# A gated linear recurrence with a convolution-gated output: deeper ring of decays, one gate tile less in flight, gated inputs on GpSimd, other written-out orders

## The chip, the cores and the metric

The kernel runs on one core of a Trainium2 chip. A core has five engines that work at the same time, each through its own queue in order: TensorE (PE, matrix products and transposes), VectorE (DVE), ScalarE (ACT), GpSimd (POOL) and SyncE (SP), which here only issues data transfers (DMAs). They work on a memory of 128 partitions (SBUF); matrix products land in eight banks of a second memory (PSUM). The metric is the device time of one execution in microseconds, as the median of several runs.

## The reference, cut to what matters

```python
# first part: x, r_gate, i_gate are (4, 6336, 256), a_param is (256,)
a_base = sigmoid(a_param)
a_t    = exp(8.0 * sigmoid(r_gate) * log(clip(a_base, 1e-6, 1 - 1e-6)))
norm   = sqrt(maximum(1.0 - a_t * a_t, 1e-6))
xg     = norm * sigmoid(i_gate) * x
h = 0
for t in range(S):                 # for each of the 4 sequences, each of 256 channels
    h = a_t[:, t] * h + xg[:, t]
    y[:, t] = h
# second part, on y
gate_pre[t] = sum(conv_w[k] * y[t - 4 + k] for k in range(5))   # zero before a sequence starts
out = (sigmoid(gate_pre) * (y @ w_val)) @ w_out                 # both weights are 256 x 256
```

## The kernel before, in words

The 4 x 6336 = 25344 tokens are one long row. It is cut into 51 tiles of 512 tokens (three of 256: the first and the last two) and into 28 chunks, nearly all of two tiles, so 1024 tokens; chunk c holds tiles 2c - 2 and 2c - 1. Every sigmoid is written as a tanh: sigmoid(z) = (1 + tanh(z/2)) / 2, so tanh and exp share one activation table, and only the square root needs another. Chunks are therefore taken in pairs (UNITS): one table load, one root for the pair, one table load back.

A tile goes through these steps; the name is the one in the planner, the letter the one in the written-out orders:

- `load` (l, SP, line 264): two DMAs of 512 KB, r_gate and i_gate, into a tile `ri` of a pool with NIN buffers. `loadx` (x, line 271): one DMA of x into `xt`, NX buffers. Both are issued on SP, as the stores are.
- `tanh` (t, ACT, line 348): both gates at once, into `tring`, which has NTR = 3 slots for r and NTI = 5 for i.
- `srT` (r, PE, line 373), per chunk and half of the channels: transposes of tanh(r) into a PSUM bank, so that channels lie on partitions. `exp` (e, ACT, line 382): the decay a_t, into `aring`, a ring of NS windows of 512 tokens.
- `e` (e, POOL, line 390): a_t squared, into `ering`. `sq` (q, ACT, line 394): the root, for a whole unit.
- `u2` (u, line 359 on DVE or lines 363 and 364 on POOL): the gated input (1 + tanh(i/2)) * x, into `uring`. On DVE it is two instructions of 128x512 that each read `tring` and `xt`; on POOL it is an add into `t1` and a product. The string U2 says which engine does which tile.
- `nT` (n, PE, line 404): transposes of the root back to tokens on partitions; `xg` (x, DVE, line 411): root times gated input; `xT` (x, PE, line 420): transposes to channels on partitions.
- `scan` (s, DVE, line 438), per chunk and half: the recurrence, reading `aring` and the bank, into `yring`.
- `conv` (c, PE, line 464): the convolution as products with diagonal matrices; `tg` (g, ACT, line 472): tanh of it; `val` (v, PE, line 480): y @ w_val; `gv` (v, DVE, line 490): their product; `out` (o, PE, line 502), two pieces per tile; `osb` (o, line 513 on DVE or 515 on ACT, by the string OSB): eviction of a piece; `store` (s, SP, line 520).

What each step waits for is written in `make_jobs` (lines 132 to 180), with a cost for each step. The lines on which ring depths act:

```python
        job("load", "DMA", f, [("tanh", g - NIN)])
        job("loadx", "DMA", f, [("u2", g - NX)])
        job("tanh", "ACT", f, [("load", g), ("u2", g - NTI)]
            + ([("srT", 2 * sh.chunk_of[g - NTR] + 1)] if g >= NTR else []))
...
            aold = ("scan", 2 * sh.aold[c] + h if sh.aold[c] >= 0 else -1)
            job("exp", "ACT", f, [("srT", k), aold])
            job("e", "POOL", f, [("exp", k), ("sq", eu), ("nT", sh.chunks[ed][3] - 1 if ed >= 0 else -1)])
```

`sh.aold[c]` is the last earlier chunk whose place in `aring` chunk c takes; with NS = 10 that is five chunks of 1024 back. The order of the work on each engine is not found while the kernel is built: it is written out as one string of letters per engine (ORDER), and BANK_ORDER gives the PSUM bank (one of four) of each srT, nT, xT and out in turn. `make_plan` walks the strings with the costs only to merge the five queues into one program order; on the chip each engine follows its own string, and waits for the others by semaphores.

Of the kernel before, what the change touches and what calls it, by code (L numbers as in the profile page):

```python
# [15 lines left out]

CHUNKS = [[256], [512]] + [[512, 512]] * 23 + [[512], [256], [256]]

UNITS = [2, 2, 2, 2, 2, 2, 2, 2, 2, 2, 2, 2, 2, 2]
NS = 10  # L20
NE = 10
NU = 10
NY = 6
NIN = 4
NX = 4
NTR = 3
NTI = 5
# [2 lines left out]
BANKS = 4  # L30
PB = dict(srT=2, nT=2, xT=2, ops=2)

OSB = "DDDDDDDDDDDDDDDDDDDDDDDDDDDDDDDDDDDDDDDDDDDDDDDDDDDDDADDDDDDDDDDDDDDDDDDDDAAAAADDDDDAAAAAAAAAAADADA"

U2 = "DDDDPDPDDPPPPPPPPPPPDPPPPPPPPPPPPPPPPPPPPPPPPPPPPPP"

COST = dict(load=(0.05, 2.72), loadx=(0.02, 1.37), tanh=(0.11, 1.7), u2P=(0.2, 3.25), u2D=(0.2, 1.7), srT=(0.05,
            0.47), exp=(0.26, 0.86), e=(0.06, 1.83), sq=(0.2, 1.71), nT=(0.05, 0.53), xg=(0.02,
            0.58), xT=(0.04, 0.46), scan=(0.13, 2.14), conv=(0.15, 1.08), tg=(0.1, 0.83), val=(0.02,
            0.88), gv=(0.07, 1.07), out=(0.02, 0.43), osbD=(0.6, 0), osbA=(0.5, 0), store=(0.03,  # L40
# [3 lines left out]
LETTERS = dict(  # L44
    DMA=dict(l="load", x="loadx", s="store"), ACT=dict(t="tanh", e="exp", q="sq", g="tg", o="osb"),
    PE=dict(r="srT", n="nT", x="xT", c="conv", v="val", o="out"), POOL=dict(e="e", u="u2"),
    DVE=dict(u="u2", x="xg", s="scan", v="gv", o="osb"))
ORDER = dict(
    DMA=("lllxlllxlxlxxlxlxxlllxxlxlxsxxlsxlxllssxxlslxsxsllxxlsxssllslsxxxlsllssxslxlslsxxsllxslxslsxxsxslllx"
         "slxsxssllxlxxsxsslslxllsxsxsxllsxslxssxsxxsssssssssss"),  # L50
    ACT=("teeteetqtteteetetgqteegtteettgqgetegetetgqgteegttgetegtgeqgteetgetgqgetettgeegtgqeegttgtegetgtegqegt"
         "tgeetgtegqegttegetgoetgqegttegetgqgetegtgetgetgqeogetgootgoeoteegeqgeogeoqogogoogogooooggoo"),
    PE=("rrrrrrnxnrxrcxvxrcvrnnxnrxrnoocxxvcornrnvnocorxronvcxvooxcxronnvrocnovxncrvxroocxrocvooxvocrononcxrn"
        "voroxconvxocvornonnrcvonxrxvorcoxocovroxvxcrvnooncooxvrocxrvocnnoorcoovxcoorvnxvonocrxvrocoxvnrocono"
        "vxoxcrvonnocxrrxvoocnnrxcovroxovconvonnxrxcrnovcxroocvoxooovcrnnonxocxrvcrvoncovoxocovronxvrnncxnovo"
        "cxroovxrrcorovxoocovnonrcxrovonxcxnnvxocovocxxovcoxovooxcovcovoo"),
    POOL="eeeeeeeeueueeeuuueeeeuuuueeeueuuueeeeuueeeeuuueeuueeuueueueeueueueueeuueueeuuueeueeuuueueeeeuueeeuu",
    DVE=("uxsuxsussuvxuxusxsvxooussovxxvxoosxovsvoosoxxsovoxvxssoovsoovosovooxxusxvoosoxvsooxoxvxvxossovoosoov"
         "svsxooxvoosvosoxovoxoovsoovxsoxvosvoosovxoxovossxxovossoxxvsovosovxooxvxssxovsoovoosoovxxoxsovsvxoov"
         "oosovxsxxvsxvsvsoovoosoxxvsvxsxxvssvssvsvsovvo"))  # L60
BANK_ORDER = ("2123321110130102331302130221230122302301230123012121132131023123012102312123210310103201301301320131"
              "2023103130123102130231201213202310203123132010303132031321023031231202302001302313021231120312310321"
              "20131232130321320112030212312010312032010301231210212310312231")

WEIGHTS_AFTER = ("e", 1)
TABLE, SEM, DMA_LAT = 1.3, 0.15, 2.2
# [2 lines left out]
BF16 = mybir.dt.bfloat16  # L69
ACT = mybir.ActivationFunctionType  # L70
ALU = mybir.AluOpType


class Shape:
# [3 lines left out]
    def __init__(self, total, seq):  # L78
# [9 lines left out]
        assert t == total  # L88
        self.apos, self.aold = self.place(NS * WIN)
        self.epos, _ = self.place(NE * WIN)  # L90
# [3 lines left out]
        self.runs, self.npos, batch_of = [], [], []  # L94
        for u, n in enumerate(UNITS):
            runs = []
# [35 lines left out]
def make_jobs(sh):  # L132
# [4 lines left out]
    jobs = {op: [] for ops in LETTERS.values() for op in ops.values()}  # L137
    unit_of = [u for u, n in enumerate(UNITS) for _ in range(n)]
    ends = [sum(UNITS[:u + 1]) for u in range(len(UNITS))]
    qlast = [max(q for q, (w, _) in enumerate(sh.pieces) if w == g) for g in range(len(sh.tiles))]  # L140

    def job(op, eng, f, deps, cost=None, bank=0):
        fix, per = COST[cost or op]
        jobs[op].append((eng, fix + per * f, [d for d in deps if d[1] >= 0], bank))

    for g, (_, n) in enumerate(sh.tiles):
        f = n / WIN
        c = sh.chunk_of[g]
# [4 lines that stand above are left out]
        job("u2", "DVE" if U2[g] == "D" else "POOL", f, [("tanh", g), ("loadx", g)] + ([("xT", 2 * sh.chunk_of[g - NU] + 1)] if g >= NU else []), "u2" + U2[g])  # L153
        job("nT", "PE", f, [("sq", unit_of[c]), ("xg", g - PB["nT"])], None, 1)
        job("xg", "DVE", f, [("nT", g), ("u2", g)])
        job("conv", "PE", f, [("scan", 2 * c + 1), ("tg", g - 1)])
        job("tg", "ACT", f, [("conv", g), ("gv", g - 2)])
        job("val", "PE", f, [("scan", 2 * c + 1), ("gv", g - 1), ("conv", g)])
        job("gv", "DVE", f, [("tg", g), ("val", g)] + ([("out", qlast[g - 2])] if g >= 2 else []))
        job("store", "DMA", f, [("osb", q) for q, (w, _) in enumerate(sh.pieces) if w == g])  # L160
    for c, (_, n, g0, g1) in enumerate(sh.chunks):
# [3 lines left out]
        for h in range(2):  # L165
            k = 2 * c + h
            job("srT", "PE", f, [("tanh", g1 - 1), ("exp", k - PB["srT"])], None, 1)
# [3 lines that stand above are left out]
            job("xT", "PE", f, [("xg", g1 - 1), ("scan", k - PB["xT"])], None, 1)  # L171
            job("scan", "DVE", f, [("xT", k), ("val", ylast - 1), ("conv", ylast)])
    for q, (g, i) in enumerate(sh.pieces):
        job("out", "PE", 1, [("gv", g), ("osb", q - PB["ops"])], None, 1)
        job("osb", "DVE" if OSB[q] == "D" else "ACT", 1, [("out", q), ("store", g - NOSB)], "osb" + OSB[q])
    for u, n in enumerate(UNITS):
        size = sum(sh.chunks[c][1] for c in range(ends[u] - n, ends[u])) / CHUNK
        fix, per = COST["sq"]
        jobs["sq"].append(("ACT", fix * len(sh.runs[u]) + per * size, [("e", 2 * ends[u] - 1)], 0))
# [3 lines left out]
def make_plan(sh):  # L183
# [5 lines left out]
    for eng, letters in ORDER.items():  # L189
        todo = {op: [i for i, job in enumerate(jobs[op]) if job[0] == eng] for op in LETTERS[eng].values()}  # L190
        seq[eng] = [(op, todo[op].pop(0)) for op in (LETTERS[eng][x] for x in letters)]
        assert not any(todo.values())
    free_bank = iter(BANK_ORDER)
    for op, i in seq["PE"]:
# [5 lines left out]
    done, order, mode = {}, [], "E"  # L200
    free = dict(dict.fromkeys(seq, 0.0), DMA=START, ACT=ACT_START)
    at, left = dict.fromkeys(seq, 0), sum(len(ops) for ops in seq.values())
    while left:
        was = left
        for eng, ops in seq.items():
            while at[eng] < len(ops):
# [9 lines left out]
                free[eng] = t + dur  # L216
                done[op, i] = t + dur + (DMA_LAT if eng == "DMA" else 0.0)
                order.append((t, op, i, eng, dur))
# [8 lines left out]
def kernel(  # L227
# [31 lines left out]
    def load(g):  # L259
        t0, nt = tiles[g]  # L260
        nj = nt // P
        ri = inp.tile([P, 2, SUB, D], FP32, name="ri", tag="ri", bufs=NIN)
        for k, src in enumerate((rf, if_)):
# [10 lines left out]
    with tc.manual_schedule():  # L274
# [51 lines left out]

        aring = rings.tile([P, H, NS * WIN], FP32, name="aring")

# [241 lines left out]
```

## Time and profile before

| what | value |
|---|---|
| time, median of 5 runs | 311.66 us (310.82 to 314.27) |
| the profiled execution | 313.02 us, of it span from first to last instruction 311.2 us |
| ACT busy | 289.1 us |
| DVE busy | 271.6 us |
| PE busy | 249.7 us |
| POOL busy | 243.8 us |
| moved by DMA | 104.51 MB, 336 GB/s over the span |
| granted TensorE clock, mean | 0.962 |

The profile is of one execution. Its page gives the busy time of each engine, then groups of instructions by line, engine and tile with the idle time before them, and what ended that idle time. In a row such as `out<-in 128x1024 f32` the tiles written and read stand ahead of their shape. Rows of the timeline give start, duration, engine and line; two neighbouring instructions of one kind are merged (x2). Consecutive ACT rows overlap by about 0.1 us[...]. "issue" as a releaser means that the profile shows nothing that the engine waited for. Idle time of an engine costs nothing by itself; it counts where another engine, or the end, waits for it.

### The profile page before, as it was taken

How to read it: one execution, taken by the hardware profiler on the slowest of the kernel's cores; microseconds unless marked ns; L12 is line 12 of the kernel's file. 1: busy time of each engine (PE TensorE's matmuls, PEld its weight loads, DVE VectorE, ACT ScalarE, POOL GpSimd, SP SyncE). 2: the span in 40 equal slices, each digit the busy share in tenths (PEclk: the TensorE clock that was granted, in tenths of full speed). 3: DMA queues.
4: the chain of work that ended last, by engine and by line, in shares of the span. 5: the costliest groups of instructions: out<-in, count | busy, mean ns of one | idle time of the engine just before them, and what ended most of it. 6: DMA issues, size and time to landing. Idle time of an engine off the chain costs nothing.

```text
span 311.2 us, 6605 instructions
## 1 busy us (share of the span) xinstructions
PE 249.7 (80%) x2591; PEld 162.5 (52%) x2591; DVE 271.6 (87%) x279; ACT 289.1 (93%) x225; POOL 243.8 (78%) x154
## 2 busy tenths in 40 slices
PE   1126564799799868989799899888897999999994
PEld 1115243465566445655566466555564766656563
DVE  3008957989999998999999999999999999999973
ACT  6799699999999995999999999999999999999762
POOL 1907719999998998548999999999999989987300
PEclk9999796979899995999999999999999999999999
DMA  7999989999898999599999999997989999673145
GB/s 200 385 372 389 400 311 413 395 349 414 293 358 319 379 347 409 197 353 420 384 331 358 359 419 417 414 417 275 393 316 336 368 418 412 238 263 136 70 181 227
DMA packets 30797, 104.51 MB, mean 336 GB/s; under 512 B 4391, under 2 KB 4654, under 8 KB 30766
## 3 DMA queue, kind: packets, MB, share of 16 engines
q1 hardware_dynamic: 29376, 103.82, 88.1%
q0 software_dynamic: 1376, 0.26, 1.0%
q8 instruction: 20, 0.33, 0.4%
q14 instruction: 11, 0.09, 0.1%
q10 hardware_dynamic: 14, 0.01, 0.0%
HBM read 78.39 MB, written 25.95 MB: 335 GB/s over the span
## 4 chain that ended last, share of the span: by engine, by line
ACT 30%; POOL 15%; issue 14%; DVE 14%; PE 14%; DMA 11%; SPq 1%; ACTq 0%; DVEq 0%; POOLq 0%
ACT tring L348 8%; POOL uring L364 8%; ACT ering L394 6%; ACT aring L382 5%; ACT tg L472 5%; DMA ri<-in_i_gate_dram 5%; DMA xt<-in_x_dram 5%; DVE yring L438 5%; PE gp L464 4%; POOL ering L390 4%; POOL t L363 4%; PE bank L502 3%; DVE gv L490 3%; ACT L394 2%; DVE uring L359 2%
## 5 line engine op out<-in xcount | busy, mean ns | idle before, releaser
L390 POOL TENSOR_TENSOR ering<-aring 128x1024 f32<-128x1024 f32 (+2 forms) x56 | 95.5, 1719 | 41.0 <-ACT aring L382 39.2
L438 DVE TENSOR_TENSOR_SCAN yring<-aring,yring,bank 128x1024 bf16<-128x1024 f32 (+5 forms) x54 | 109.9, 2048 | 3.4 <-PE bank L420 3.4
L364 POOL TENSOR_TENSOR uring<-t,xt 128x1024 bf16<-128x1024 f32 (+1 forms) x43 | 100.0, 2327 | 3.6
L348 ACT ACTIVATE tring<-ri 128x2048 bf16<-128x2048 f32 (+1 forms) x51 | 94.2, 1867 | 4.2 <-issue 2.6
L464 PE MATMUL gp<-yring,diag 64*64 64x512 bf16 (+15 forms) x1196 | 67.6, 354 | 1.3 <-ACT tg L472 0.7
L382 ACT ACTIVATE aring<-bank,khf 128x1024 f32<-128x1024 bf16 (+2 forms) x56 | 61.0, 1109 | 4.1 <-PE bank L373 3.4
L502 PE MATMUL bank<-wo,gv 128*128 128x256 bf16 x396 | 58.7, 276 | 6.5 <-DVE osb L513 2.1
L490 DVE SCALAR_TENSOR_TENSOR gv<-tg,val 128x1024 bf16<-128x1024 bf16 (+1 forms) x54 | 60.3, 1120 | 3.2 <-PE val L480 2.5
L373 PE MATMUL bank<-ident_b,tring 128*128 128x128 bf16 x396 | 36.4, 240 | 27.0 <-ACT tring L348 19.1
L472 ACT ACTIVATE tg<-gp 128x1024 bf16<-128x1024 f32 (+1 forms) x51 | 51.3, 1006 | 5.1 <-PE gp L464 4.3
L480 PE MATMUL val<-yring,wv 128*128 128x512 bf16 (+1 forms) x204 | 52.4, 380 | 3.1 <-DVE gv L490 3.0
L513 DVE TENSOR_SCALAR osb<-bank 128x512 f32<-128x512 f32 x80 | 52.4, 676 | 2.3 <-PE bank L502 2.1
L502 PEld LDWEIGHTS <-gv 128*128 128x128 bf16 x396 | 36.8, 99 | 24.1 <-issue 10.1
L373 PEld LDWEIGHTS <-tring 128*128 128x128 bf16 x396 | 29.5, 108 | 35.2 <-ACT tring L348 20.7
L411 DVE TENSOR_TENSOR uring<-bank,uring 128x1024 bf16<-128x1024 bf16 (+1 forms) x51 | 33.4, 664 | 16.2 <-PE bank L404 15.8
L394 ACT ACTIVATE ering<-ering,b 128x4096 bf16<-128x4096 f32 (+4 forms) x16 | 46.8, 2934 | 0.2
L363 POOL TENSOR_SCALAR t<-tring 128x1024 f32<-128x1024 bf16 (+1 forms) x43 | 45.0, 1047 | 1.7
L404 PE MATMUL bank<-ident_f,ering 128*128 128x128 f32 x198 | 36.1, 311 | 11.4 <-ACT ering L394 3.7
L464 PEld LDWEIGHTS <-diag 64*64 64x64 bf16 x1196 | 30.0, 109 | 27.4 <-issue 12.5
L404 PEld LDWEIGHTS bank<-ident_f,ering 128*128 128x128 f32 x198 | 28.5, 208 | 19.1 <-ACT ering L394 8.0
L420 PE MATMUL bank<-ident_f,uring 128*128 128x128 f32 x198 | 33.6, 289 | 5.1 <-DVE uring L411 2.4
L420 PEld LDWEIGHTS bank<-ident_f,uring 128*128 128x128 f32 x198 | 22.8, 145 | 16.0 <-DVE uring L411 4.4
(32 smaller groups left out, 105.8 us busy)
## 6 DMA issues: line engine op xcount, KB each, us to landing
ri<-in_r_gate_dram SPq DMA_DIRECT2D x48, 512.0 KB, 7.8
ri<-in_i_gate_dram SPq DMA_DIRECT2D x48, 512.0 KB, 8.5
xt<-in_x_dram SPq DMA_DIRECT2D x48, 512.0 KB, 8.6
out_dram<-osb SPq DMA_DIRECT2D x48, 512.0 KB, 6.3
ri<-in_r_gate_dram SPq DMA_DIRECT2D x3, 256.0 KB, 6.1
ri<-in_i_gate_dram SPq DMA_DIRECT2D x3, 256.0 KB, 7.6
xt<-in_x_dram SPq DMA_DIRECT2D x3, 256.0 KB, 5.2
out_dram<-osb SPq DMA_DIRECT2D x3, 256.0 KB, 2.1
```

The costliest lines, as they stand in the source:

```text
L348: nc.scalar.activation(out=tring[:, r:i + 1:i - r, 0:nj, :], in_=ri[:, :, 0:nj, :], func=ACT.Tanh, scale=0.5)
L364: nc.gpsimd.tensor_tensor(out=u.rearrange("p w d e -> p w e d"), in0=t1.rearrange("p (w e) d -> p w e d", e=2), in1=xt.rearrange("p (w e) ...
L373: nc.tensor.transpose(out=srT[:, col:col + P], in_=tring[:, g % NTR, j, h * P:(h + 1) * P], identity=ident_b[:])
L382: nc.scalar.activation(out=aring[:, h, a0:a0 + nt].rearrange("c (w p j) -> c w p j", p=P, j=nj), in_=live.pop(("srT", k))[:, 0:nt].rearran ...
L390: nc.gpsimd.tensor_tensor(out=ering[:, H * e0 + h * nt:H * e0 + (h + 1) * nt], in0=a, in1=a, op=ALU.mult)
L394: nc.scalar.activation(out=nring[:, 2 * H * e0:2 * H * e0 + H * m], in_=ering[:, H * e0:H * (e0 + m)], func=ACT.Sqrt, scale=-0.25, bias=b0 ...
L404: nc.tensor.transpose(out=nT[:, w * D + h * P:w * D + (h + 1) * P], in_=ering[:, n0 + w:n0 + nw * P:nw], identity=ident_f[:])
L438: nc.vector.tensor_tensor_scan(out=yring[:, h, y0 + c0:y0 + c1], data0=aring[:, h, a0 + c0:a0 + c1], data1=xT[:, c0:c1], initial=0.0 if fr ...
L464: nc.tensor.matmul(out=gp[64 * h:64 * h + 64, m, c0:c1], lhsT=diag[rows, h, kk, rows], rhs=yring[rows, h, src:src + c1 - c0], start=(sh == 0),
L472: nc.scalar.activation(out=tg[:, :, 0:nt], in_=live.pop(("gp", g))[:, :, 0:nt], func=ACT.Tanh, scale=0.5)
L490: nc.vector.scalar_tensor_tensor(out=gv[:, 0:nj, hs, :].rearrange("c j h p -> c j (h p)"), in0=tg[:, hs, 0:nt].rearrange("c h (p j) -> c j ...
L502: nc.tensor.matmul(out=ops[:, e * D:(e + 1) * D], lhsT=gv[:, 2 * i + e, hk, :], rhs=wo[:, hk, :], start=(hk == 0), stop=(hk == H - 1))
```

## The change

Six constants and the order strings are replaced. No instruction's form changes.

- NS from 10 to 12: `aring` holds 1024 tokens more. NIN from 4 to 3: one tile of gates less.
- U2: on DVE were tiles 0, 1, 2, 3, 5, 7, 8 and 20 (D); now tiles 0, 1, 2, 4 and 8.
- UNITS: the last two roots cover 1 and 3 chunks instead of 2 and 2; the last root thus covers 512 + 256 + 256 tokens instead of 256 + 256.
- OSB: 18 evictions on ACT instead of 19, at other pieces.
- The planner's cost of a gated input on DVE, and the strings of all five queues and of the banks.

```diff
@@ -16,12 +16,12 @@
 
 CHUNKS = [[256], [512]] + [[512, 512]] * 23 + [[512], [256], [256]]
 
-UNITS = [2, 2, 2, 2, 2, 2, 2, 2, 2, 2, 2, 2, 2, 2]
-NS = 10
+UNITS = [2, 2, 2, 2, 2, 2, 2, 2, 2, 2, 2, 2, 1, 3]
+NS = 12
 NE = 10
 NU = 10
 NY = 6
-NIN = 4
+NIN = 3
 NX = 4
 NTR = 3
 NTI = 5
@@ -30,11 +30,11 @@
 BANKS = 4
 PB = dict(srT=2, nT=2, xT=2, ops=2)
 
-OSB = "DDDDDDDDDDDDDDDDDDDDDDDDDDDDDDDDDDDDDDDDDDDDDDDDDDDDDADDDDDDDDDDDDDDDDDDDDAAAAADDDDDAAAAAAAAAAADADA"
-
-U2 = "DDDDPDPDDPPPPPPPPPPPDPPPPPPPPPPPPPPPPPPPPPPPPPPPPPP"
-
-COST = dict(load=(0.05, 2.72), loadx=(0.02, 1.37), tanh=(0.11, 1.7), u2P=(0.2, 3.25), u2D=(0.2, 1.7), srT=(0.05,
+OSB = "DDDDDDDDDDDDDDDDDDDDDDDDDDDDDDDDDDDDDDDDDDDDDDDDDDDDDDDDDDDDDDDDDDDDDDDAADADADDDDADDAAAAAAADAAAAADA"
+
+U2 = "DDDPDPPPDPPPPPPPPPPPPPPPPPPPPPPPPPPPPPPPPPPPPPPPPPP"
+
+COST = dict(load=(0.05, 2.72), loadx=(0.02, 1.37), tanh=(0.11, 1.7), u2P=(0.2, 3.25), u2D=(0.3, 3.3), srT=(0.05,
             0.47), exp=(0.26, 0.86), e=(0.06, 1.83), sq=(0.2, 1.71), nT=(0.05, 0.53), xg=(0.02,
             0.58), xT=(0.04, 0.46), scan=(0.13, 2.14), conv=(0.15, 1.08), tg=(0.1, 0.83), val=(0.02,
             0.88), gv=(0.07, 1.07), out=(0.02, 0.43), osbD=(0.6, 0), osbA=(0.5, 0), store=(0.03,
@@ -46,21 +46,22 @@
     PE=dict(r="srT", n="nT", x="xT", c="conv", v="val", o="out"), POOL=dict(e="e", u="u2"),
     DVE=dict(u="u2", x="xg", s="scan", v="gv", o="osb"))
 ORDER = dict(
-    DMA=("lllxlllxlxlxxlxlxxlllxxlxlxsxxlsxlxllssxxlslxsxsllxxlsxssllslsxxxlsllssxslxlslsxxsllxslxslsxxsxslllx"
-         "slxsxssllxlxxsxsslslxllsxsxsxllsxslxssxsxxsssssssssss"),
-    ACT=("teeteetqtteteetetgqteegtteettgqgetegetetgqgteegttgetegtgeqgteetgetgqgetettgeegtgqeegttgtegetgtegqegt"
-         "tgeetgtegqegttegetgoetgqegttegetgqgetegtgetgetgqeogetgootgoeoteegeqgeogeoqogogoogogooooggoo"),
-    PE=("rrrrrrnxnrxrcxvxrcvrnnxnrxrnoocxxvcornrnvnocorxronvcxvooxcxronnvrocnovxncrvxroocxrocvooxvocrononcxrn"
-        "voroxconvxocvornonnrcvonxrxvorcoxocovroxvxcrvnooncooxvrocxrvocnnoorcoovxcoorvnxvonocrxvrocoxvnrocono"
-        "vxoxcrvonnocxrrxvoocnnrxcovroxovconvonnxrxcrnovcxroocvoxooovcrnnonxocxrvcrvoncovoxocovronxvrnncxnovo"
-        "cxroovxrrcorovxoocovnonrcxrovonxcxnnvxocovocxxovcoxovooxcovcovoo"),
-    POOL="eeeeeeeeueueeeuuueeeeuuuueeeueuuueeeeuueeeeuuueeuueeuueueueeueueueueeuueueeuuueeueeuuueueeeeuueeeuu",
-    DVE=("uxsuxsussuvxuxusxsvxooussovxxvxoosxovsvoosoxxsovoxvxssoovsoovosovooxxusxvoosoxvsooxoxvxvxossovoosoov"
-         "svsxooxvoosvosoxovoxoovsoovxsoxvosvoosovxoxovossxxovossoxxvsovosovxooxvxssxovsoovoosoovxxoxsovsvxoov"
-         "oosovxsxxvsxvsvsoovoosoxxvsvxsxxvssvssvsvsovvo"))
-BANK_ORDER = ("2123321110130102331302130221230122302301230123012121132131023123012102312123210310103201301301320131"
-              "2023103130123102130231201213202310203123132010303132031321023031231202302001302313021231120312310321"
-              "20131232130321320112030212312010312032010301231210212310312231")
+    DMA=("lllxxlllxllxxlxxlxlxlxsllxlxsxlxlslxslxxsllsslxxlslxsxlsxxsllsxlxssllxslxlsxlsxxslxssllsxxxslslslxls"
+         "xxsslxllxsxlsxslslxslssxsxlxxslxlslxsxsssxssssxssssss"),
+    ACT=("teteeetqttgeteetegtqetteeetgtgqteetgtegtetgeegqtgtetegetqgetgteegtgqgtgeteetgtegeetgqtgteegtgqegttge"
+         "etgetgqgteegttgeetgeqgetgtgtegetgqetgtegeetgoqogotgetgoeteegeteegqeogqogoogoogogogooogogoo"),
+    PE=("rrrrnnxxcrvrxxrcrrovnnxrxornrcovncxrxorvnncxnvnrocxrvoocroovxrcvxoocnnoovnxrrncoxrvoxooxcvnnrocoxvno"
+        "rrcnoxcovxorvconnoxcovroxvrncnrxocvroorocvooxcxovonnvxrxrconocnovxorcvroxvonconvorocoxvrnxcoovncooxv"
+        "rxoocrnnvoxocrrvconnxrovrooxcovnnxcovnxcoxrcvnrocoovooxvrxcnvonroocorxvrcooxnoovncxxovnnocnroxcvornx"
+        "rcrxvrrocrovoroxvcovnnocooxvxnoocxovoncovxcoxvncxooxvoxocovcovoo"),
+    POOL=("eeeeeeeeuueueeeuuueueueeeueuueeuuueeeeuuuueeueeuueeueeuuueueeeuuueeueeuueueueeuueueeeuuuueueeeeueeeu"
+          "uu"),
+    DVE=("uuxxssssvuuoxxvsosxuvxososvxxsxxovsovooovssovoxooxxsxvosovoossxxvoosxvoxosovsovoxxosovosxvxsoovoovoo"
+         "sovosxxvssooxxovosvosovxoxoovosxvsxoovoososvxxoovosvoxxsovoosoxxvsxovsosovxoovoosvsxoxovoosvoosxxvso"
+         "sxvxxosvxssvoovoovsxxovosxvsvsxvssvxsosvsvvo"))
+BANK_ORDER = ("3103031221330332022130201023120302012320130210301021031302130302123302101302130213023102102103203023"
+              "1302332031010021320312021302101201231032031012301210301323023123021321320132013212012302102310210312"
+              "30121031201312031203210230131203213013021331210213023103120010")
 
 WEIGHTS_AFTER = ("e", 1)
 TABLE, SEM, DMA_LAT = 1.3, 0.15, 2.2
```

The ACT order from the start to root 3, spelled out with numbers (t tanh and g tg by tile, e exp by half chunk, q root by unit), before and after:

```
before  t0 e0 e1 t1 e2 e3 t2 q0 t3 t4 e4 t5 e5 e6 t6 e7 t7 g0 q1 t8 e8 e9 g1 t9 t10 e10 e11 t11 t12 g2 q2
        g3 e12 t13 e13 g4 e14 t14 e15 t15 g5 q3
after   t0 e0 t1 e1 e2 e3 t2 q0 t3 t4 g0 e4 t5 e5 e6 t6 e7 g1 t7 q1 e8 t8 t9 e9 e10 e11 t10 g2 t11 g3 q2
        t12 e12 e13 t13 g4 t14 e14 g5 t15 e15 t16 g6 e16 e17 g7 q3
```

From root 5 to root 6:

```
before  q5 g14 e24 t24 e25 t25 t26 g15 e26 e27 g16 t27 g17 q6
after   q5 g14 t24 g15 e24 t25 e25 e26 t26 g16 t27 e27 g17 e28 e29 t28 g18 q6
```

The start of GpSimd's order (e square by half chunk, u gated input by tile):

```
before  e0 .. e7 u4 e8 u6 e9 e10 e11 u9 u10 u11 e12 e13 e14 e15 u12
after   e0 .. e7 u3 u5 e8 u6 e9 e10 e11 u7 u9 u10 e12 u11 e13 u12 e14 e15
```

The orders of SP, PE and DVE and the banks are other strings of the same letters.

## The prediction

> **What bounds the kernel now.** I read the busy shares first, then ScalarE's waits, then the order of time around its two long waits. The shares are columns engine, busy us, share, instructions:
>
> ```profile
> PE 249.7 (80%) x2591; PEld 162.5 (52%) x2591; DVE 271.6 (87%) x279; ACT 289.1 (93%) x225; POOL 243.8 (78%) x154
> ```
>
> Busy shares by stage say more: between 160 and 200 us ACT works 39.88 of 40, DVE 39.53, POOL 39.16, PE 36.89. ACT is the tightest and its work hardly changes, so the time is 289 us of ACT plus the holes in ACT. ScalarE's own waits (us in total, times, longest):
>
> ```profile
> ACT tg L472 <- PE gp L464: 4.3, 5, 1.5
> ACT aring L382 <- PE bank L373: 3.4, 3, 2.4
> ACT tring L348 <- issue: 2.6, 1, 2.6
> ```
>
> Between 20 and 280 us only three holes matter: 2.63 at 31.3, 2.42 at 116.5, 0.99 at 122.0; the rest lies before 13 us or after 290. No hole there is a wait for a load, and none is a wait for POOL. The late pair in order of time (start, duration, engine, line, what, [idle before]):
>
> ```profile
> 110.34 2.38 POOL L364 TENSOR_TENSOR uring<-t,xt 128x1024 bf16<-128x1024 f32 x1
> 110.58 5.00 DVE L359 SCALAR_TENSOR_TENSOR uring<-tring,xt 128x512 bf16<-128x512 bf16 x2
> 117.90 1.01 PE L373 MATMUL bank<-ident_b,tring 128*128 128x128 bf16 x8 [3.43 <-DVE yring L438]
> 118.95 1.20 ACT L382 ACTIVATE aring<-bank,khf 128x1024 f32<-128x1024 bf16 x1 [2.42 <-PE bank L373]
> 120.55 2.35 PE L464 MATMUL gp<-yring,diag 64*64 64x512 bf16 x20
> 122.95 1.02 ACT L472 ACTIVATE tg<-gp 128x1024 bf16<-128x1024 f32 x1 [0.99 <-PE gp L464]
> ```
>
> The gated input of tile 20 holds VectorE for 5.00 us beside a busy GpSimd. The scan behind it ends at 117.85, PE waited 3.43 us for that scan's bank, and ACT waited for PE. The convolution that follows took 2.35 us for 20 matmuls instead of 1.27 (the granted clock between 116 and 124 us is 0.57) and makes the 0.99. So 3.41 us of ACT hang on one operation. The early hole:
>
> ```profile
> 29.29 4.52 DVE L359 SCALAR_TENSOR_TENSOR uring<-tring,xt 128x512 bf16<-128x512 bf16 x2
> 33.89 1.91 ACT L348 ACTIVATE tring<-ri 128x2048 bf16<-128x2048 f32 x1 [2.63 <-issue]
> 34.80 2.35 POOL L364 TENSOR_TENSOR uring<-t,xt 128x1024 bf16<-128x1024 f32 x1
> 42.75 1.31 DVE L359 SCALAR_TENSOR_TENSOR uring<-tring,xt 128x512 bf16<-128x512 bf16 x2
> 45.70 1.94 POOL L390 TENSOR_TENSOR ering<-aring 128x1024 f32<-128x1024 f32 x1 [8.55 <-ACT aring L382]
> ```
>
> The pair of 4.52 us is the gated input of tile 2; it ends at 33.81, and tanh 7, which overwrites that gate's slot (NTI = 5), starts at 33.89. Again it is a gated input on VectorE.
>
> **Gated inputs moved (tiles 3, 5, 7, 20 to GpSimd, tile 4 to VectorE).** On GpSimd one costs L363 plus L364, 1.07 + 2.38 = 3.45 us. On VectorE it cost 1.31 (POOL idle) to 5.00 us. The Trainium skill, GPSIMD Engine Reference, "Engine selection", speaks against the move: a two-input elementwise operation belongs on VectorE and is about 2x slower on GpSimd. The row of 1.31 agrees (2.6x), and by it three more tiles would cost 3 x (3.45 - 1.31) = 6.4 us of engine time for nothing. The row of 5.00, taken beside a working GpSimd, says that tile 20 is the cheaper one on GpSimd. I go by the rows: VectorE sheds 2.23 + 1.31 + 1.31 + 5.00 = 9.9 us, takes back about 4.5 for tile 4 (GpSimd squares at 27 to 33 us, so the 4.52 row is the near one) and 0.7 for one more eviction: 4.7 us less. ACT loses one eviction, 0.5.
> GpSimd gets 3 x 3.45 = 10.3 us more. Tiles 3 and 5 are queued behind square 7, where POOL now idles 8.55 us after tile 4's product: they end near 41 us, and square 8 comes near 43. Tile 7 is queued ahead of tile 9, so squares 12 and later slip; yet summing POOL's queue up to square 11, tiles 10 and 7 included, gives about 64 us, and the root that needs square 15 is due near 81, its square done near 79. Behind a late square stands that root, and ACT with it; the margin is 2 us there and 5 or more later, since POOL idles 8 us between 129 and 141 now. Cost taken: 0; if that cover is gone, up to 2 us once.
> What is saved: the 3.41 us at 116 to 123. In the start ACT's new order puts conv-gate tanh 0 and 1 ahead of tanh 7, and tile 2's product comes up after gv 0, near 25 to 29.5 us, ahead of tanh 7 near 33 to 35. Next late there is the transpose of chunk 3, which stands behind convolution 1 on PE; I leave 0.6 for it and count 2.0 of 2.63.
>
> **Ring of decays, 10 to 12 windows.** No instruction is added. An exp may run six chunks ahead of its scan instead of five. ACT was never held by that ring, so it yields nothing by itself. The new order uses it: exps 28 and 29 now stand before root 6, so GpSimd has squares to do during the 6.3 us of a root.
>
> **Gate tiles, 4 to 3.** Loads keep count and bytes. Each one waits for tanh g-3 instead of g-4, on SP's queue, with x loads and stores behind it. The ACT work from the end of that tanh to the start of tanh g is the window in which the load has to land. Steps come from these ACT rows, start to start:
>
> ```profile
> 42.62 1.91 ACT L348 ACTIVATE tring<-ri 128x2048 bf16<-128x2048 f32 x1
> 44.44 2.28 ACT L382 ACTIVATE aring<-bank,khf 128x1024 f32<-128x1024 bf16 x2
> 46.61 1.02 ACT L472 ACTIVATE tg<-gp 128x1024 bf16<-128x1024 f32 x1
> 47.52 3.71 ACT L348 ACTIVATE tring<-ri 128x2048 bf16<-128x2048 f32 x2
> 51.12 2.30 ACT L382 ACTIVATE aring<-bank,khf 128x1024 f32<-128x1024 bf16 x2
> ```
>
> Tanh 1.80, exp 1.09, tg 0.91; a root with its two table loads 6.3 (36.30 to 42.62). Before, the windows have a median of 19.6 us and, past the fill, the shortest are 10.2 and 10.6. In the new order the median is 15.6, and eight fall under 9: tiles 6, 11, 15, 16, 20, 27, 35, 43 with 7.3, 7.7, 8.6, 7.5, 8.6, 8.6, 8.6, 8.4 (tile 15: e12 e13 t13 g4 t14 e14 g5 = 3 x 1.09 + 2 x 1.80 + 2 x 0.91 = 8.7, less the 0.1 by which a row outlasts its step). In all eight the stores and x loads ahead of the load in SP's order belong to tiles whose evictions and products ACT's own progress already requires, so SP adds nothing. How long a load takes is the unknown: the page's median and the shortest-window load of before (tile 12, issued the moment its slot came free):
>
> ```profile
> ri<-in_i_gate_dram SPq DMA_DIRECT2D x48, 512.0 KB, 8.5
> DMA to landing us min/median/max: 6.9/6.9/6.9
> ```
>
> With 0.5 for the first half's issue ahead, that is 9.0 and 7.4. At 7.4 the windows fall short by 0.1 us in all; at 8.1 by 1.8; at 9.0 by 6.7. Loads released straight into a free slot (5.4, 6.9, 7.0 and 7.8 to landing) lie nearer the low end, and the tight tiles are of that kind. I take just under 8: 1.2 us.
>
> **The end.** Root 13 now covers the last 1024 tokens instead of 512. ACT work up to its end is 275.7 us in the old order and 273.3 in the new (from tanh 0, by the steps): 2.4 earlier. What PE still has to do after it grows by one tile's convolution (1.27), two output pieces (1.06) and some transposes, together 3.2. PE is dense there (9.56 of 10 us between 290 and 300), so the end loses 0.8 net.
>
> **Sum.** -3.4 - 2.0 + 1.2 + 0.8 = -3.4 us. The profiled execution took 313.02 (span 311.2 and 1.8 around it), so 309.6; it lies 1.4 above the median of the runs, 311.66, so against that 308.3. A change under 1% (3.1 us) is what this measurement can hardly tell from none.
>
> **Rivals.**
> *Slower: the load becomes the bound.* If a gate load takes 9.0 us or more from the release to its landing also in the tight windows, ACT waits in them. The 4.6 us gained without it are used up at 8.7 us; at 9.4 the shortage is 10 us, and the kernel is slower by over 1.5%, some 317. For it: the page's median of 8.5, and DMA busy at 88% of the span. Against: the direct releases above, and fewer loads stand in the queue at once.
> *No change: shorter lag, new waits.* The new order leaves 25.5 us of ACT work from root 5 to the conv gate of tile 18, the old one 30.0. The chain between (transposes, two scans, convolution among VectorE's queue) I sum to 16.5 after the root ends. The slack is about 4 us, so a slow stretch would hold ACT for some tenths per pair of chunks; 13 x 0.25 = 3.3 takes the gain: 311.5.
> *A larger gain.* Loads never late and the start's 2.63 fully gone: 306.5; with two of the tail's small waits gone as well, 305.
> *It doesn't do what it says*: ACT never waited for decays to be scanned, so the ring alone gives 0; that is in the sum.
>
> **Chances.** Forecast (306.8 to 309.8) 0.48, larger gain 0.12, no change 0.22, slower by the loads 0.18. The forecast lies at the 1% line (308.5), so about 0.7 of it counts as faster: faster 0.46, same 0.34, slower 0.20. Range 304.5 to 314.5: from the larger gain to loads at some 9.1 us.
>
> **What would show it.** No DVE L359 row after 60 us; no ACT hole between 110 and 125; tanh 7 waiting under 1 us; waits "ACT tring <- DMA ri" of about 1 us in total, at the eight tiles named. POOL busy near 254, DVE near 267. I am wrong if ACT waits more than 5 us for ri, or for PE in many small pieces between 130 and 280.

## The result and the profile after

| | before | after |
|---|---|---|
| median | 312.21 us (76 runs, 310.4 to 314.27) | 310.13 us (39 runs, 308.13 to 313.39) |
| ratio | 1 | 0.9927, 95% interval 0.9913 to 0.9941 |
| profiled execution, of it span | 313.02, 311.2 us | 312.07, 310.3 us |

The kernel became 0.73% faster, 2.3 us (1.8 to 2.7). The ratio leaves out executions over 1.5% above the fastest of their kernel, so it is a little lower than that of the two medians. Forecast were 1.1%, 3.4 us (308.3 against a median of 311.66): the sign and the range hold, and the gain was put half as large again as it is. On the prediction's own base the measured time is 0.9927 x 311.66 = 309.4 us, inside its 306.8 to 309.8. The prediction held that a change under 1% can hardly be told from none; the interval here is 0.14% to either side. The profiled execution of after has a span of 310.3 us; a second one of the same kernel, used below, has 307.8.

The busy times of after, from its page:

```profile
PE 248.2 (80%) x2591; PEld 165.1 (53%) x2591; DVE 267.0 (86%) x274; ACT 288.9 (93%) x224; POOL 253.5 (82%) x160
```

VectorE 267 and GpSimd 254 are what was forecast from the rows of the moved gated inputs. What changed lies in ScalarE's waits (us in total, times, longest):

```profile
ACT tg L473 <- PE gp L465: 4.6, 5, 1.5
ACT aring L383 <- PE bank L374: 2.7, 4, 1.2
...
ACT ering L395 <- POOL ering L391: 2.2, 1, 2.2
ACT tring L349 <- DMA ri<-in_i_gate_dram: 1.7, 1, 1.7
```

The 2.6 us of tanh 7 are gone. The exps' 2.7 are other waits than the 2.42 of before: they stand at 11, 26, 33 and 95 us. The 4.6 of the conv gates all lie after 288 us. The wait for a load is the one at the very start, at 7.4 us, which was there before. New is the third line: root 0 waits 2.2 us for GpSimd.

The stage in which the late pair of holes stood, 116 to 124 us, before and then after (us of the stage, then busy time of PE, PEld, DVE, ACT, POOL with the instructions, then granted clock, DMA share, GB/s):

```profile
116.00:124.00 8.00, 6.10 (x43) 3.83 (x43) 7.11 (x7) 4.57 (x5) 6.89 (x5) 0.57 1.03 412
```

```profile
116.00:124.00 8.00, 7.25 (x115) 5.17 (x113) 7.53 (x9) 7.98 (x7) 6.05 (x5) 1.00 1.00 346
```

ScalarE works 7.98 of 8 us instead of 4.57: the 3.4 us are there. The start of the kernel is where the prediction went wrong. GpSimd's order of time of before, then of after:

```profile
7.44 1.18 POOL L390 TENSOR_TENSOR ering<-aring 128x256 f32<-128x256 f32 x2 [6.13 <-ACT aring L382]
8.57 3.06 POOL L527 DMA_DIRECT2D wv<-in_moe_w_val_dram  x4
11.62 1.21 POOL L530 DMA_DIRECT2D wo<-in_moe_w_out_dram  x2
12.82 2.32 POOL L390 TENSOR_TENSOR ering<-aring 128x512 f32<-128x512 f32 x2
```

```profile
7.46 0.61 POOL L391 TENSOR_TENSOR ering<-aring 128x256 f32<-128x256 f32 x1 [6.15 <-ACT aring L383]
11.53 0.61 POOL L391 TENSOR_TENSOR ering<-aring 128x256 f32<-128x256 f32 x1 [3.46 <-ACT aring L383]
12.08 3.06 POOL L528 DMA_DIRECT2D wv<-in_moe_w_val_dram  x4
15.13 1.21 POOL L531 DMA_DIRECT2D wo<-in_moe_w_out_dram  x2
16.34 2.06 POOL L391 TENSOR_TENSOR ering<-aring 128x512 f32<-128x512 f32 x2
```

The new ScalarE order has tanh 1 ahead of exp 1, so square 1 comes at 11.5 instead of 8.0. Behind square 1, by the line WEIGHTS_AFTER, GpSimd issues the six DMAs of the weight matrices, 4.3 us of its time. Before, they lay in a gap; now squares 2 and 3 stand behind them, and so does root 0 on ScalarE:

```profile
14.96 1.28 ACT L395 ACT_TABLE_LOAD   x1
18.43 1.57 ACT L395 ACTIVATE ering<-ering,b 128x1536 bf16<-128x1536 f32 x1 [2.19 <-POOL ering L391]
```

Before, root 0 began at 16.50, straight behind its table load.

### The profile page after: what moved, and what is told of

It reads as the page before. It is cut to its first block, busy times and chain, and to the rows that moved or that the text cites. A ratio compares the mean times of both kernels' runs of the same rounds, so it can differ in the third digit from the quotient of the medians.

```text
span 310.3 us, 6621 instructions
## 1 busy us (share of the span) xinstructions
PE 248.2 (80%) x2591; PEld 165.1 (53%) x2591; DVE 267.0 (86%) x274; ACT 288.9 (93%) x224; POOL 253.5 (82%) x160
## 5 line engine op out<-in xcount | busy, mean ns | idle before, releaser
L365 POOL TENSOR_TENSOR uring<-t,xt 128x1024 bf16<-128x1024 f32 (+1 forms) x46 | 106.8, 2322 | 12.2 <-PE gp L465 8.4
L514 DVE TENSOR_SCALAR osb<-bank 128x512 f32<-128x512 f32 x81 | 53.7, 678 | 6.0 <-PE bank L503 5.6
L481 PE MATMUL val<-yring,wv 128*128 128x512 bf16 (+1 forms) x204 | 53.4, 386 | 1.5 <-DVE gv L491 1.4
L465 PEld LDWEIGHTS <-diag 64*64 64x64 bf16 x1196 | 32.3, 108 | 33.6 <-issue 18.6
L364 POOL TENSOR_SCALAR t<-tring 128x1024 f32<-128x1024 bf16 (+1 forms) x46 | 48.1, 1046 | 1.8
L395 ACT ACTIVATE ering<-ering,b 128x4096 bf16<-128x4096 f32 (+2 forms) x16 | 46.8, 2934 | 2.3 <-POOL ering L391 2.2
L405 PE MATMUL bank<-ident_f,ering 128*128 128x128 f32 x198 | 35.2, 312 | 16.7 <-ACT ering L395 13.9
L374 PE MATMUL bank<-ident_b,tring 128*128 128x128 bf16 x396 | 34.3, 230 | 13.9 <-ACT tring L349 9.8
L405 PEld LDWEIGHTS bank<-ident_f,ering 128*128 128x128 f32 x198 | 29.3, 208 | 25.9 <-ACT ering L395 17.1
L374 PEld LDWEIGHTS <-tring 128*128 128x128 bf16 x396 | 27.9, 104 | 22.1 <-ACT tring L349 11.5
```

What stands on the lines that cost most here:

```text
L365: nc.gpsimd.tensor_tensor(out=u.rearrange("p w d e -> p w e d"), in0=t1.rearrange("p (w e) d -> p w e d", e=2), in1=xt.rearrange("p (w e) ...
L374: nc.tensor.transpose(out=srT[:, col:col + P], in_=tring[:, g % NTR, j, h * P:(h + 1) * P], identity=ident_b[:])
L405: nc.tensor.transpose(out=nT[:, w * D + h * P:w * D + (h + 1) * P], in_=ering[:, n0 + w:n0 + nw * P:nw], identity=ident_f[:])
L465: nc.tensor.matmul(out=gp[64 * h:64 * h + 64, m, c0:c1], lhsT=diag[rows, h, kk, rows], rhs=yring[rows, h, src:src + c1 - c0], start=(sh == 0),
L481: nc.tensor.matmul(out=val[:, m, 0:nt], lhsT=wv[:, hk, m * P:(m + 1) * P], rhs=yring[:, hk, y0:y0 + nt], start=(hk == 0), stop=(hk == H - 1))
```

## The experiments

All ratios are to the kernel before, run beside it on the same chip.

**Tile 20's gated input alone.** The kernel before with that one product moved:

```diff
 # GpSimd's order, spelled out
-e20 e21 e22 e23 u21 u22
+e20 e21 e22 e23 u20 u21 u22
 # VectorE's order
-x14 x15 u20 s16 x16
+x14 x15 s16 x16
```

> The kernel before with one edit: the gated input of tile 20 goes from VectorE to GpSimd, queued there just ahead of tile 21; all else as before. If that one operation (5.00 us on VectorE) makes the two ScalarE holes of 2.42 and 0.99 us at 116 to 123 us, they are gone and the time is about 3.4 us shorter: ratio 0.989, and below the changed kernel's 0.993. If the holes belong to that place in the orders (a PSUM bank or a scan that would be late anyway), or GpSimd hands 3.4 us on, the ratio is 0.998 to 1.003.

Measured: 0.9916 (0.9893 to 0.9939), 309.63 us. ScalarE in order of time:

```profile
113.88 1.92 ACT L348 ACTIVATE tring<-ri 128x2048 bf16<-128x2048 f32 x1
115.68 1.03 ACT L472 ACTIVATE tg<-gp 128x1024 bf16<-128x1024 f32 x1
116.58 1.22 ACT L382 ACTIVATE aring<-bank,khf 128x1024 f32<-128x1024 bf16 x1
117.67 1.93 ACT L348 ACTIVATE tring<-ri 128x2048 bf16<-128x2048 f32 x1
```

No row has an idle time in front, so both holes are gone. The gain is 2.6 us (1.9 to 3.3), as much as the whole change brings, from one letter moved. ScalarE waits for GpSimd nowhere in this trace. The second hole goes with the granted clock from 116 to 124 us: the clock is 0.57 before, and 1.00 here and in the changed kernel. In the kernel before with the new depths (below), whose orders are the same, it is 0.79. There TensorE stands still for 2.77 us instead of 3.43, and ScalarE has only one hole at this place, of 1.76 us. That TensorE's standing still lowers the clock was not tried by itself.

**The same product back on VectorE in the changed kernel.**

```diff
 # GpSimd's order
-u19 u20 u21 u22 e24
+u19 u21 u22 e24
 # VectorE's order
-x14 x15 v10
+x14 x15 u20 v10
```

> The changed kernel with tile 20's gated input back on VectorE, right behind the product of root and gated input of tile 15, as before. If a contended gated input of 5 us on VectorE holds ScalarE wherever it stands, a hole of 2 to 3.4 us returns near 110 to 120 us: ratio to the kernel before 0.999 to 1.004. If the changed orders leave VectorE enough slack (its work is 4.6 us less, and it waits for TensorE near 90 us), the hole is under 1 us and the ratio stays at 0.993 to 0.996.

Measured: 1.0202 (1.0176 to 1.0228), 318.36 us, far outside both expectations. VectorE's row of that product, and the exp that follows on ScalarE:

```profile
116.46 1.31 DVE L360 SCALAR_TENSOR_TENSOR uring<-tring,xt 128x512 bf16<-128x512 bf16 x2 [6.77 <-DMA xt<-in_x_dram]
...
123.03 2.30 ACT L383 ACTIVATE aring<-bank,khf 128x1024 f32<-128x1024 bf16 x2 [7.59 <-PE bank L374]
```

The product itself took 1.31 us; GpSimd had run out of work at 115 us. The loss is the wait for x of tile 20, which SP's new order brings late. So this run says nothing about contention, only that 6.8 us of VectorE standing still cost ScalarE 7.6. It had to be repeated with the x loads moved as well:

```diff
 # SP's order, added to the edit above
-x17 x18 l22 s7 l23 x19 s8 x20
+x17 x18 x19 x20 l22 s7 l23 s8
```

> The changed kernel with tile 20's gated input back on VectorE as in the earlier run, and the x loads of tiles 19 and 20 issued some 7 us earlier on SP (right behind that of tile 18), so that the product does not wait for its x. If a gated input of about 5 us beside a busy GpSimd holds ScalarE also here, a hole of 2 to 4 us comes back at 113 to 120 us: ratio 0.999 to 1.006. If only the wait for x made the loss, and VectorE's slack in these orders takes up the 5 us, the ratio is 0.992 to 0.995.

Measured: 1.0061 (1.0040 to 1.0083), 314.51 us; against the changed kernel's 0.9923, measured in other runs (below), that is 1.4%, 4.3 us. Its rows in order of time:

```profile
110.46 4.51 DVE L360 SCALAR_TENSOR_TENSOR uring<-tring,xt 128x512 bf16<-128x512 bf16 x2
...
116.16 1.86 PE L481 MATMUL val<-yring,wv 128*128 128x512 bf16 x4 [3.17 <-DVE gv L491]
...
119.52 1.09 PE L374 MATMUL bank<-ident_b,tring 128*128 128x128 bf16 x16
...
120.20 2.30 ACT L383 ACTIVATE aring<-bank,khf 128x1024 f32<-128x1024 bf16 x2 [3.92 <-PE bank L374]
```

Beside a working GpSimd the product takes 4.51 us again. The gv behind it is late, PE's y @ w_val waits 3.17 for that, the transposes of tanh(r) stand behind it on PE, and ScalarE waits 3.92 for them. That VectorE has 4.6 us less to do in these orders doesn't help: it has no slack at this place. The moved x loads were not run alone; past the start, ScalarE waits 0.26 us for a gate load in this trace, so they are hardly the cost.

**The weights' DMAs.**

```diff
-WEIGHTS_AFTER = ("e", 1)
+WEIGHTS_AFTER = ("e", 0)
```

> The changed kernel with the six DMAs that fetch the two weight matrices issued on GpSimd behind square 0 instead of square 1, so at 8 us, where GpSimd idles 3.5 us. If the 2.19 us that root 0 waits comes from these 4.3 us of issuing ahead of squares 2 and 3, root 0 starts about 2 us earlier, and the time falls by as much: ratio 0.986. If what follows in the start is held by something else (the transposes of chunk 3, the loads), the 2 us are lost again before root 2: ratio 0.992.

Measured: 0.9864 (0.9842 to 0.9886), 307.66 us, some 2 us below the changed kernel. ScalarE in order of time:

```profile
15.22 1.28 ACT L395 ACT_TABLE_LOAD   x1
16.52 1.57 ACT L395 ACTIVATE ering<-ering,b 128x1536 bf16<-128x1536 f32 x1
...
54.74 1.28 ACT L395 ACT_TABLE_LOAD   x1
```

Root 0 follows its table load without a gap, and the table load of root 2 begins at 54.74 (third line). The same table load in the kernel before, then in the two traces of the changed kernel:

```profile
57.95 1.28 ACT L394 ACT_TABLE_LOAD   x1
```

```profile
58.27 1.28 ACT L395 ACT_TABLE_LOAD   x1
```

```profile
56.56 1.28 ACT L395 ACT_TABLE_LOAD   x1
```

The kernel before has a tanh more and a conv gate less done by then, 0.89 us of work, so 57.06 is what to compare with. The start is 2.3 us shorter with the weights moved; in the changed kernel it is 1.2 us longer in the first trace and 0.5 shorter in the second. The hole of 0.97 at 33 us, which only the first has, is a part of that difference.

**The two depths.** First the new orders with the old depths, then the old orders with the new depths:

```diff
 # a_old_depths and a_old_depths_2: from the changed kernel
-NS = 12
+NS = 10
-NIN = 3
+NIN = 4
```

```diff
 # b_depths: from the kernel before
-NS = 10
+NS = 12
-NIN = 4
+NIN = 3
```

> The changed kernel, its orders and its choice of engines, with the depths of before: ring of decays of 10 windows, four gate tiles. In the changed kernel's trace the exp that would come closest to a scan in a ring of 10 starts 5.9 us after that scan's end, and ScalarE waits for no load past the start. So if the depths bring nothing, the ratio is the changed kernel's, 0.993 plus or minus 0.002, in spite of the shallower ring. If the deeper ring is what the new orders live on, ScalarE waits in exps for scans and the ratio is 0.998 or more; if the fourth gate tile is worth something, it falls to 0.990.

Measured: 0.9954 (0.9939 to 0.9970), 311.0 us. That touches the changed kernel's interval only at 0.994, so it was run once more, beside the changed kernel.

> The changed kernel itself, unedited, so that the other kernels of this call can be compared with it on one chip. Expected: its own ratio, 0.993 plus or minus 0.002.

> The changed kernel with the depths of before (ring of 10 windows, four gate tiles) once more, beside the changed kernel itself. If the depths bring nothing, the two ratios agree within 0.0025, and the 0.9954 of the first run was chance. If the deeper ring or the smaller load queue is worth something that no wait in the trace shows, it is again 0.002 to 0.004 above.

> The kernel before, its orders and its choice of engines, with the two new depths alone: ring of decays of 12 windows, three gate tiles. With three gate tiles these orders leave ScalarE windows of 5.7 us (tile 12) and 7.5 us (tiles 20, 31, 36) for a load; loads that were released straight into a free slot in the changed kernel landed after 5.3 to 7.6 us. If the ring alone brings nothing and the loads behave so, ScalarE waits 1 to 3 us in all: ratio 1.003 to 1.01. If stores and x loads that stand ahead of the gate loads in these orders hold them up too (they were issued up to 17 us late with four tiles), it waits 5 us or more: ratio 1.016 or more. If the ring is the part that pays, the ratio is below 0.998.

> The kernel before with the two new depths alone, for its trace: ScalarE's waits for gate loads past 20 us are under 1 us in all, as the ratio of 1.000 says; the straight loads of tiles 12, 20, 31 and 36 land within their windows or less than 0.5 us behind.

Measured: the changed kernel 0.9923 (0.9894 to 0.9951), with the old depths 0.9884 (0.9847 to 0.9920), the kernel before with the new depths 1.0004 (0.9987 to 1.0022). The old depths came out 0.27% above the changed kernel once and 0.39% below it once; no sign holds, and these runs can't tell an effect of some tenths of a per cent from none. For the ring the trace gives the reason: with room for 12 windows no exp of the changed kernel starts less than 15.4 us after the end of the scan whose place it takes; counted for 10 windows it is still 5.9. So the new orders, exps 28 and 29 ahead of root 6 included, don't need the deeper ring: they ran with 10 windows, and no exp waits for a scan in either trace. The two depths were only changed together; that neither does anything rests on these waits. The new depths in the old orders cost nothing that the ratio shows, though I expected 1 to 3 us of load waits. ScalarE's waits in the kernel before with the new depths:

```profile
ACT tring L348 <- DVE uring L359: 2.6, 1, 2.6
ACT tring L348 <- DMA ri<-in_i_gate_dram: 2.3, 3, 1.4
```

Of the 2.3 us for loads 1.4 are at the very start. The rest, 0.9, is at 98.6 and 166.5 us. The first line names what the page of before called "issue": tanh 7 waits for VectorE's gated input, 2.6 us.

**Two gate tiles.**

```diff
-NIN = 3
+NIN = 2
```

> The changed kernel with two gate tiles in flight instead of three. The windows between the end of tanh g-2 and the start of tanh g shrink to a median of 6.8 us and a least of 3.5. If a load released into a free slot takes 6.5 us from release to landing, as the straight ones did in the changed kernel's trace (5.3 to 7.6), the shortages add up to 26 us: ratio 1.07. At 7.5 us it would be 48 us (1.14). If fewer loads in the queue make each one much faster (4 us), it is under 5 us: ratio 1.01.

Measured: 1.0849 (1.0789 to 1.0909), 338.64 us. Its first wait:

```profile
ACT tring L349 <- DMA ri<-in_i_gate_dram: 17.8, 13, 4.2
```

The prediction's rival in which loads become the bound is real one gate tile further down, and there costs 29 us against the changed kernel. Waits for loads are 17.8 of it. What the rest is, new waits of exps and conv gates for PE among it (13.5 us with those of the tail, against 7.3), I didn't follow further.

**Three moves of order together.** The weights' DMAs as above and, on PE:

```diff
-r6 c1 r7 r8
+r6 r7 c1 r8
...
-v8 n12 x12 r18 r19
+v8 r18 n12 x12 r19
```

> The changed kernel with three moves of order: the weights' DMAs issued behind square 0, on TensorE the transposes of chunk 3 (second half) ahead of the convolution of tile 1, and those of chunk 9 (first half) ahead of the root transposes of tile 12. If the ScalarE holes of 2.19, 0.97 and 1.19 us in the changed kernel's trace add up, the time falls by 4 us against it: ratio 0.980. If the two small holes come and go with the granted clock from run to run, only the first counts: ratio 0.986, as with the weights alone.

Measured: 0.9840 (0.9813 to 0.9867), 307.68 us. The interval overlaps that of the weights alone, so only the first move is shown to count in the time. In the trace the transposes of chunk 3 (r7) moved ahead of the convolution of tile 1 (c1) do what they should: the granted clock from 28 to 36 us is 0.61, lower than in the changed kernel's traces, and ScalarE has no hole there. Both this kernel and the one with the weights alone beat the changed kernel and the one before.

The holes of 0.97 at 33 and 1.19 at 95 us are not in every execution of the changed kernel. PE's convolution of tile 1 in the profile first shown, then in the other execution:

```profile
30.77 2.34 PE L465 MATMUL gp<-yring,diag 64*64 64x512 bf16 x19 [0.66 <-DVE yring L439]
```

```profile
30.40 1.27 PE L465 MATMUL gp<-yring,diag 64*64 64x512 bf16 x19 [0.65 <-DVE yring L439]
```

The same 19 matmuls take 2.34 and 1.27 us; the granted clock from 28 to 36 us is 0.79 in the one and 1.00 in the other, and only the first has the hole behind it. From 88 to 98 us the clock is 0.66 and 0.85, and again only the first has the hole. The two holes make 2.2 of the 2.5 us by which these two spans differ, less the 0.47 us for a load that only the second has; that the clock is the cause wasn't tried by itself.

## Why the prediction was right in part

- **Tile 20 and the holes at 116 to 123 us: right.** 3.4 was forecast and 3.4 is what the stage shows; as a time it is 2.6 (1.9 to 3.3), and putting the product back costs 4.3. The 3.41 us are of one execution; the 1.76 of another with the same orders show that the size of this hole changes from one to the next.
- **GpSimd's 10.3 us more at no cost: right.** ScalarE waits for GpSimd once, in root 0, and not for a gated input.
- **VectorE's busy time: right, with luck.** The gated inputs of tiles 2 and 4 took 6.61 us together, where 4.52 and about 4.5 were counted. That of tile 8, which was not moved and was counted as unchanged, took 4.48 us instead of 2.51. The two errors nearly cancel in the 267 us. None of the three held ScalarE for long.

```profile
56.16 2.51 DVE L359 SCALAR_TENSOR_TENSOR uring<-tring,xt 128x512 bf16<-128x512 bf16 x2
```

```profile
31.27 6.61 DVE L360 SCALAR_TENSOR_TENSOR uring<-tring,xt 128x512 bf16<-128x512 bf16 x4
...
52.96 4.48 DVE L360 SCALAR_TENSOR_TENSOR uring<-tring,xt 128x512 bf16<-128x512 bf16 x2
```

- **The start: the step that failed.** I counted 2.0 of tanh 7's 2.63 as saved. That part came true: tanh 7 follows the conv gate of tile 1 at once (second and third line; the first has the transposes of chunk 3, for which 0.6 was left: 0.97 in this trace, none in the second).

```profile
33.98 1.20 ACT L383 ACTIVATE aring<-bank,khf 128x1024 f32<-128x1024 bf16 x1 [0.97 <-PE bank L374]
35.08 1.01 ACT L473 ACTIVATE tg<-gp 128x1024 bf16<-128x1024 f32 x1
35.98 1.91 ACT L349 ACTIVATE tring<-ri 128x2048 bf16<-128x2048 f32 x1
```

But the order also exchanges tanh 1 and exp 1. The prediction does not follow that exchange to GpSimd, where the weights' six DMAs are tied to square 1, and so puts its cost at nothing. The DMAs moved 3.5 us later, over squares 2 and 3, and root 0 paid 2.19. Moving them back gives some 2 us. With this row, L527 and L530, followed past square 1 the sum is -3.4 - 2.0 + 2.2 + 1.2 + 0.8 = -1.2, and with the loads at no cost -2.4, against 2.3 measured. That it comes so close is partly luck: tile 20 alone brought 2.6 and not 3.4, and the start differs by 1.7 us between the two traces.
- **Loads: mechanism right, price too high.** The tight windows are there, and none costs anything to speak of: under 0.1 us in the first trace, 0.47 at tile 16 in the second. The three tightest, of tiles 6, 11 and 16, came out at 7.7 to 8.2 us, wider than the 7.3 to 7.7 forecast. Tile 16's own load, by the profile of after, issued to landed:

```profile
DMA to landing us min/median/max: 7.2/7.2/7.2
```

 With 0.4 for the first half's issue that is 7.6 in a window of 7.7. The tight ones of tiles 27, 35 and 43 landed 5.3, 6.4 and 6.7 us after their release in windows of 8.4 to 8.6; in the second trace it was 6.5, 7.2 and 6.7. Just under 8 had been taken.
- **The end: right.** From the end of root 13 to the end of the span it is 22.2 us before (289.02 to 311.17) and 25.2 after (285.09 to 310.3), 3.1 more; 3.2 was forecast. Root 13 of before, then of after:

```profile
287.87 1.15 ACT L394 ACTIVATE ering<-ering,b 128x1024 bf16<-128x1024 f32 x1
```

```profile
283.09 2.00 ACT L395 ACTIVATE ering<-ering,b 128x2048 bf16<-128x2048 f32 x1
```

- **Shorter lag, new waits: small.** Between 40 and 280 us the holes come to 1.6 us in the first trace, and in the second to little more than the 0.47 for a load.

## What to carry to other kernels

When an order is changed, follow each moved instruction on every queue, with what is tied to it: here six DMA issues on GpSimd, tied to one small instruction, took back most of what the start had gained. Where three engines work 39 of 40 us, one operation that takes 5 us instead of 1.3 can reach the bounding engine within a few steps, whatever the sum of busy times seems to leave. It need not: tile 20's did, tile 8's 4.48 us in the changed kernel did not, so the rows behind it have to be followed. Before a buffer is deepened or given away, read its distances from the trace (a load's window against its landing, a ring's reuse against its last reader). Here they say that a ring of 10 windows still has 6 us to spare, and that with two gate tiles the windows get shorter than the loads; the run with two then lost 29 us.

## What the runs showed of the hardware

The gated input on VectorE, two instructions that each read two SBUF tiles, takes 1.31 us with GpSimd idle. With GpSimd at work it takes 2.51 us (tile 8 before), 4.48 (tile 8 after), 4.51 and 5.00 (tile 20). DMA traffic is not what differs: at the 1.31 us of before, from 42.75 us on, the DMA share is 0.90, at the 5.00 us it is 0.96. The two squares on GpSimd beside the product of 4.51 us took 4.68 instead of 3.74. The loss is on both sides. What sets a pair to 2.5 or to 5 us was not followed.

The six weight DMAs cost GpSimd 4.3 us of its own queue to issue (4 x 0.77 and 2 x 0.61).

The time of a gate load from issue to landing, median over all of them, is 8.0 us before, 7.4 in the changed kernel and 6.2 with two gate tiles. That is not the depth alone. In the changed kernel with four gate tiles it is 7.6 and 7.5, against 7.4 and 7.5 with three, so in these orders the step from four to three shows nothing. With two the DMAs also moved less, 331 GB/s against 359 from 40 to 280 us.
